# The softmax weights' row sums: adding the constant and scaling on ScalarE instead of VectorE

## The chip, the cores and the metric

The kernel runs on one core of a Trainium2 chip. The metric is the device time of one execution in microseconds; the time before is the median of three runs. One execution was also taken by the hardware profiler; its trace is what the line numbers and durations below are from.

The engines are called TensorE (PE; its weight loads are PEld), VectorE (DVE), ScalarE (ACT), GpSimd (POOL) and SyncE (SP). Each runs its own queue of instructions in order and waits for the others by semaphores.

## The reference

Causal attention with a cumulative bias, followed by a feed-forward network. Batch 8, 8 heads, 576 positions, head dimension 64; the network goes from 512 to 2048 and back, over all 4608 tokens.

```
scores = scale * q @ k.T + min(-(cum[i] - cum[j]), 0)     # causal; cum = cumsum(max(s, 0))
scores = scores - max(scores)
attn   = exp(scores)
attn   = attn / (sum(attn) + 1e-09)
x      = attn @ v                                          # heads side by side: 4608 x 512
h      = x @ w_in
g      = h if h >= 1, 0 if h <= -1, else (h + 1)**2 / 4
out    = g @ w_out
```

## The kernel before

Precision first, since it explains most of the instructions: each operand of a large product is split into a high and a low half-precision part, and three products (high-high, low-high, high-low) are added up in PSUM. The splits are the work of VectorE, ScalarE and GpSimd.

**Attention** goes by pairs of heads: 8 batches with 4 pairs each. Each pair has two jobs, one for the first 320 rows (three row tiles of 64, 128 and 128 rows) and one for the last 256 (two row tiles of 128). For each batch there come four jobs of the first kind and then four of the second. A job is cut into eight slots (`att_slot`): preparation of q and k, the score units, the loading of the next job, and, one job later, the product with v (`att_out`).

A score unit (`scores`) makes one row tile of one head: the matmuls (lines 408, or 411 and 412 from the thirteenth job on), a VectorE pass that adds the mask and finds the row's minimum (line 417), and a ScalarE exponential that also accumulates the row sum into one column of the tile `sm` (line 428). The profile shows the exponential as two instructions: the activation, and the read of the accumulator. When both heads of a row tile are there, `weights_t` turns the exponentials into weights:

- line 444, VectorE: `rs = (sums + EPS) * 2^-12` on a tile of two columns, one per head;
- line 445, VectorE: the reciprocal of `rs`;
- line 449, GpSimd: the first head's weights, times `rs`, to half precision;
- line 450, ScalarE: the second head's exponentials times `rs`, in place;
- lines 451 and 452, GpSimd: high and low part of the second head;
- line 455, VectorE: low part of the first head, and behind it SP's DMA that transposes the tile into `pt`. This last step is put off (`late`) until behind the next score minimum.

There are 32 pairs with 5 row tiles, so 160 calls of `weights_t`.

**The feed-forward network** goes over steps of one batch half and one of 16 blocks of 128 hidden columns. `ffn_h` makes 12 matmuls into PSUM (line 528), a ScalarE ReLU (line 540), two VectorE passes (543, 544), a ScalarE copy to half precision (554) and a GpSimd subtraction (555); `ffn_y` makes 12 matmuls into four accumulating banks (line 567).

**The weights** come as pairs of 32-bit words. `Weights.decode` and `Weights.split` rebuild and split them on ScalarE, VectorE and GpSimd (lines 200 to 237) while the first attention jobs and the first FFN steps run; line 207 is a ScalarE identity activation with a bias tile. The second weights' loads (`wor`) reuse buffers that the decoding frees.

**The order on each engine** isn't the program's. The kernel is built with a planner (`schedule_with_timeline_sim=True`) that simulates the engines and picks, among the instructions that are ready in its simulation, by program order and by the priorities that the kernel gives (`tc.high_priority` for lines 417, 485, 486, 540 to 555 and 581, and for the second weights' decoding). The result is a fixed queue for each engine.

Of the kernel before, what the change touches and what calls it, by code (L numbers as in the profile page):

```python
# [9 lines left out]
F32 = mybir.dt.float32  # L10
# [4 lines left out]
AF = mybir.ActivationFunctionType  # L15
ALU = mybir.AluOpType
# [6 lines left out]
P = 128  # L23
# [9 lines left out]
EPS = 1e-9  # L33
# [40 lines left out]
def attention_ffn(ctx: ExitStack, tc: tile.TileContext, qT, kT, vT, s, w_in, w_out, yT):  # L74
    nc = tc.nc
    LOADQ, CUMQ, FIRSTQ = nc.sync, nc.scalar, nc.sync
    V, A, G, T = nc.vector, nc.scalar, nc.gpsimd, nc.tensor

    cp = ctx.enter_context(tc.tile_pool(name="cp", bufs=1))
# [7 lines left out]

    floor_bias = cp.tile([P, 1], F32, name="floor_bias")
    V.memset(floor_bias, -31.0 / 64.0)

    def pow2floor(out, in_, least):
        V.tensor_scalar(out, in_, least, None, ALU.max)
        V.tensor_scalar(out.bitcast(I32), out.bitcast(I32), 0x7F800000, None, ALU.bitwise_and)
# [218 lines left out]
    raws, pts_, vts, pbs, sums = {}, {}, {}, {}, {}  # L312
# [80 lines left out]
    def scores(n, i, hd, c0, c1):  # L393
# [37 lines left out]
        if hd:  # L431
            weights_t(n, i)

    def weights_t(n, i):

        off, R, W = QT[i]
        hf = 0 if i < 3 else 1
        h_off, N, tiles = HALF[hf]
        if i == tiles[0]:
            pts_[n, hf] = ap.tile([P, 4 * (tiles[-1] + 1), N], F16, tag="pt", bufs=2, name=f"pt{n}_{hf}")  # L440
        PT = pts_[n, hf]
        PB = ap.tile([P, i + 1, 4, P], F16, tag=f"pb{hf}", name=f"pb{n}_{i}")
        rs = ap.tile([P, 2], F32, tag="rs", bufs=4, name=f"rs{n}_{i}")
        V.tensor_scalar(rs[:R], sums.pop((n, i))[:R], EPS, 2.0 ** -12, ALU.add, ALU.mult)
        V.reciprocal(rs[:R], rs[:R])  # L445
        tiles2 = pbs.pop((n, i))
        pv, pw = (Pt[:R, :W + D].rearrange("p (j c) -> p j c", c=P) for Pt in tiles2)
        his, los = ([PB[:R, :, 2 * hd + l, :] for hd in range(2)] for l in range(2))
        G.tensor_scalar(his[0], pv, rs[:R, :1], 1.0, ALU.mult, ALU.mult)  # L449
        A.activation(tiles2[1][:R, :W], tiles2[1][:R, :W], AF.Copy, scale=rs[:R, 1:])  # L450
        G.tensor_scalar(his[1], pw, 1.0, 1.0, ALU.mult, ALU.mult)  # L451
        G.tensor_tensor(los[1], pw, his[1], ALU.subtract)  # L452

        def rest():
            V.scalar_tensor_tensor(los[0], pv, rs[:R, :1], his[0], ALU.mult, ALU.subtract)  # L455
            nc.sync.dma_start_transpose(
                out=PT[:, :4 * (i + 1), off - h_off:off - h_off + R],
                in_=PB[:R].rearrange("p j g c -> p (j g c)"),
            )

        late.append(rest)
# [226 lines left out]
```

## Time and profile before

| | before |
|---|---|
| median of three runs | 1112.76 us (1111.5 to 1112.82) |
| the profiled execution: time | 1112.3 us |
| the profiled execution: span of the trace | 1110.2 us |
| mean granted TensorE clock | 0.982 |
| softmax row tiles (calls of `weights_t`) | 160 |

The span goes from the first to the last instruction; the 2.1 us between span and time lie around it. A row of a group reads: line, engine, operation, written tile <- read tiles, shapes, count | busy us, mean ns of one | idle time of the engine just before them, and what ended it. A row of a stretch gives, for each engine, the busy time in that stretch and the number of instructions. "The chain" is the work that ended last, followed back from the last instruction: at each step to what released it, or to the instruction before it on its engine; "issue" in it is time in which the engine waited for nothing that the profile shows.

### The profile page before, as it was taken

To read this page: it belongs to the slowest core of one execution; us is meant where nothing else is said; L and a number is where in the kernel's file an instruction comes from. 1 tells how busy PE (TensorE), PEld (TensorE's weight loads), DVE (VectorE), ACT (ScalarE), POOL (GpSimd) and SP (SyncE) were. 2 spreads that over 40 slices of the span, in tenths; PEclk is the share of its full clock that TensorE was granted. 3 is DMA by queue.
4 is the path that set the end of the run, shared out by engine and by line. 5 is a ranking of instruction groups with operands and counts; after the bars stand their busy time and mean duration, and the time that the engine had idled before them with its cause. 6 is when DMAs were issued, how large, how long until landed. Compare 5 with 4: busy or idle time off the path is not lost.

```text
span 1110.2 us, 25043 instructions
## 1 busy us (share of the span) xinstructions
PE 999.0 (90%) x8470; PEld 771.2 (69%) x8470; DVE 855.0 (77%) x2392; ACT 715.9 (64%) x1683; POOL 657.2 (59%) x1161
## 2 busy tenths in 40 slices
PE   0454799899999999999999999999999999899998
PEld 0132466588767877777777877787777877787787
DVE  7979987578868877878787877787777886887533
ACT  3647766467557775777567775877576755777432
POOL 3666275676647664766566755766476665765522
PEclk9997899699999999999999999999999999999999
DMA  8984536767638763987558763977387874666300
GB/s 257 241 174 129 186 78 126 140 120 152 127 84 187 165 151 72 181 164 158 106 119 186 156 149 74 193 155 167 68 178 155 170 129 80 152 156 138 68 24 20
DMA packets 339623, 153.70 MB, mean 138 GB/s; under 512 B 290728, under 2 KB 321320, under 8 KB 339496
## 3 DMA queue, kind: packets, MB, share of 16 engines
q1 hardware_dynamic: 329792, 142.17, 60.2%
q10 hardware_dynamic: 9704, 9.93, 2.9%
q8 instruction: 67, 1.10, 0.4%
q14 instruction: 60, 0.49, 0.1%
HBM read 71.00 MB, written 9.73 MB: 73 GB/s over the span
## 4 chain that ended last, share of the span: by engine, by line
PE 61%; DVE 15%; DMA 7%; POOL 7%; issue 6%; ACT 4%; ACTq 0%; DVEq 0%; SPq 0%; POOLq 0%
PE h L528 25%; PE y L567 24%; PE px L474 4%; DMA pt<-pb 4%; PE s L411 3%; DVE pb L455 3%; PE s L412 3%; DVE p L417 2%; POOL pb L449 2%; DVE Q1s L362 1%; ACT u L540 1%; PE s L408 1%; DMA wor<-in_moe_w_out_dram 1%; POOL pb L452 1%; DVE h L543 1%
## 5 line engine op out<-in xcount | busy, mean ns | idle before, releaser
L528 PE MATMUL h<-x,WI 128*128 128x256 f16 (+1 forms) x3072 | 463.5, 290 | 22.2 <-DVE u L544 19.6
L567 PE MATMUL y<-g,WO 128*128 128x256 f16 (+1 forms) x3072 | 453.0, 287 | 8.4 <-POOL g L555 6.5
L528 PEld LDWEIGHTS <-WI 128*128 128x128 f16 x3072 | 291.2, 99 | 116.3 <-issue 27.9
L567 PEld LDWEIGHTS <-WO 128*128 128x128 f16 x3072 | 288.1, 98 | 93.4 <-issue 13.8
L555 POOL TENSOR_TENSOR g<-u,g 128x320 f16<-128x320 f32 (+1 forms) x256 | 204.5, 799 | 161.2 <-ACT g L554 156.1
L428 ACT ACTIVATE p<-p,mn 64x64 f32<-64x64 f32 (+4 forms) x320 | 179.5, 561 | 140.2 <-DVE mn L417 123.0
L540 ACT ACTIVATE u<-h,ub,us 128x320 f32<-128x320 f32 (+1 forms) x256 | 149.3, 583 | 121.6 <-PE h L528 119.7
L543 DVE SCALAR_TENSOR_TENSOR h<-h,ws,u 128x320 f32<-128x320 f32 (+1 forms) x256 | 132.4, 517 | 96.9 <-ACT u L540 94.4
L449 POOL TENSOR_SCALAR pb<-p,rs 64x128 f16<-64x128 f32 (+4 forms) x160 | 95.3, 595 | 173.3 <-DVE rs L445 108.0
L452 POOL TENSOR_TENSOR pb<-p,pb 64x128 f16<-64x128 f32 (+4 forms) x160 | 169.1, 1057 | 9.3
L455 DVE SCALAR_TENSOR_TENSOR pb<-p,rs,pb 64x128 f16<-64x128 f32 (+4 forms) x160 | 132.3, 827 | 44.9 <-POOL pb L449 44.7
L417 DVE CUSTOM_DVE_ANT_0 p<-s,mask 64x64 f32<-64x64 f32 (+4 forms) x320 | 134.6, 421 | 33.5 <-PE s L412 17.4
L544 DVE SCALAR_TENSOR_TENSOR u<-u,r,h 128x320 f32<-128x320 f32 (+1 forms) x256 | 130.2, 509 | 6.2
L411 PE MATMUL s<-K1s,Q1s 128*128 128x288 f32 (+4 forms) x312 | 117.5, 378 | 11.4 <-DVE Q1s L362 7.1
L450 ACT ACTIVATE p<-p,rs 64x64 f32<-64x64 f32 (+4 forms) x160 | 89.5, 559 | 58.9 <-DVE rs L445 57.7
L554 ACT CAST g<-u 128x320 f16<-128x320 f32 (+1 forms) x256 | 108.1, 422 | 9.8 <-DVE u L544 9.1
L451 POOL TENSOR_SCALAR pb<-p 64x128 f16<-64x128 f32 (+4 forms) x160 | 93.9, 587 | 11.8 <-ACT p L450 10.0
L412 PE MATMUL s<-K2s,Q2s 68*128 68x288 f32 (+4 forms) x312 | 95.9, 307 | 1.1 <-DMA K2s<-cumd 0.7
L474 PEld LDWEIGHTS <-vt 128*64 128x64 f16 x1536 | 74.0, 115 | 32.9 <-issue 17.9
L474 PE MATMUL px<-pt,vt 128*64 128x256 f16 (+3 forms) x1536 | 84.1, 262 | 10.8 <-DMA pt<-pb 6.8
L411 PEld LDWEIGHTS s<-K1s,Q1s 128*128 128x128 f32 (+1 forms) x312 | 56.6, 181 | 21.2 <-issue 6.7
L363 DVE TENSOR_TENSOR K2s<-rk,K1s 64x1152 fp32r<-64x1152 f32 (+1 forms) x52 | 59.1, 1136 | 2.2 <-ACT K1s L360 0.9
(123 smaller groups left out, 963.3 us busy)
## 6 DMA issues: line engine op xcount, KB each, us to landing
rk<-in_k_dram SPq DMA_DIRECT2D x56, 288.0 KB
v<-in_v_dram SPq DMA_DIRECT2D x32, 288.0 KB
wir<-in_moe_w_in_dram SPq DMA_DIRECT2D x16, 512.0 KB
wor<-in_moe_w_out_dram SPq DMA_DIRECT2D x16, 512.0 KB
rk<-in_k_dram SPq DMA_DIRECT2D x48, 160.0 KB
rq<-in_q_dram SPq DMA_DIRECT2D x48, 160.0 KB
rq<-in_q_dram SPq DMA_DIRECT2D x56, 128.0 KB
out_dram<-o ACTq DMA_DIRECT2D x32, 160.0 KB
```

What stands on the lines that cost most here:

```text
L411: T.matmul(sc[:R, :c1 - c0], Q1[:, hd, qo:qo + R], K1[:, hd, c0:c1], start=True, stop=False)
L417: ttr[0] = V.tensor_tensor_reduce(out=Pt[:R, c0:c1], in0=sc[:R, :c1 - c0], in1=mask[:R, mo:mo + c1 - c0], scale=-0.125, scalar=3.0e38 if m ...
L428: A.activation(Pt[:R, :W], Pt[:R, :W], AF.Exp, bias=m2[:R], scale=-1.0, accum_out=sums[n, i][:R, hd:hd + 1])
L452: G.tensor_tensor(los[1], pw, his[1], ALU.subtract)
L455: V.scalar_tensor_tensor(los[0], pv, rs[:R, :1], his[0], ALU.mult, ALU.subtract)
L474: T.matmul(px[hd * D:(hd + 1) * D, lo:N], VT[:, vl * NB + j, hd * D:(hd + 1) * D], PT[:, 4 * j + 2 * hd + pl, lo:], start=(m == 0), stop=( ...
L528: T.matmul(h[:, :N], WI[4 * kt + ft // 4][:, wl, ft % 4 * P:(ft % 4 + 1) * P], x[:, kt, xl], start=(n == 0), stop=(n == 3 * NKT - 1),)
L540: first = A.activation(u, h[:, :N], AF.Relu, bias=ubi[b], scale=usc[b]).ins
L543: V.scalar_tensor_tensor(h[:, :N], h[:, :N], wsc[b], u, ALU.mult, ALU.max)
L544: V.scalar_tensor_tensor(u, u, r, h[:, :N], ALU.min, ALU.mult)
L555: G.tensor_tensor(g[:, 1], u, g[:, 0], ALU.subtract)
L567: T.matmul(ys[b, hf, m][:, :N], WO[8 * (m // 2) + ft // 2][:, wl, c0:c0 + P], g[:, gl], start=(ft == 0 and n == 0), stop=(ft == NFT - 1 an ...
```

## The change

Line 444 moves from VectorE to ScalarE. The activation computes `identity(scale * in + bias)`, so the constant is scaled beforehand and kept in a tile of one column, which a VectorE memset fills at the start of the kernel. The reciprocal and everything behind it stay where they are. With three lines added, the lines behind it move down by three in the kernel after.

```
     floor_bias = cp.tile([P, 1], F32, name="floor_bias")
     V.memset(floor_bias, -31.0 / 64.0)
+
+    eps_bias = cp.tile([P, 1], F32, name="eps_bias")
+    V.memset(eps_bias, EPS * 2.0 ** -12)
...
         rs = ap.tile([P, 2], F32, tag="rs", bufs=4, name=f"rs{n}_{i}")
-        V.tensor_scalar(rs[:R], sums.pop((n, i))[:R], EPS, 2.0 ** -12, ALU.add, ALU.mult)
+        A.activation(rs[:R], sums.pop((n, i))[:R], AF.Identity, bias=eps_bias[:R], scale=2.0 ** -12)
         V.reciprocal(rs[:R], rs[:R])
```

## The prediction

> **What bounds the kernel now.** I read the page first (busy shares, the chain that ended last), then the busy time by stretches, the groups of instructions, the chain in two stretches and the order of time around single instructions.
>
> ```profile
> span 1110.2 us, 25043 instructions
> PE 999.0 (90%) x8470; PEld 771.2 (69%) x8470; DVE 855.0 (77%) x2392; ACT 715.9 (64%) x1683; POOL 657.2 (59%) x1161
> PE 61%; DVE 15%; DMA 7%; POOL 7%; issue 6%; ACT 4%; ACTq 0%; DVEq 0%; SPq 0%; POOLq 0%
> ...
> 0.00:240.00 240.00, 154.30 (x972) 101.75 (x973) 193.38 (x556) 144.96 (x308) 137.26 (x233) 0.91 0.67 161
> 240.00:1040.00 800.00, 778.43 (x6921) 614.34 (x6919) 637.45 (x1789) 547.78 (x1324) 501.48 (x905) 1.00 0.67 142
> ```
>
> In the stretches the columns after the length are PE, PEld, DVE, ACT, POOL, then the granted clock. The kernel has two lives. In the first 240 us PE is idle for 86 us: weights are decoded, and VectorE is busy for 193 of 240 us. From 240 to 1040 us PE is idle for only 22 of 800 us, so nothing done to another engine can win more than 22 us there. Behind 1040 us no softmax is left for the change to touch. In the middle the 22 us are not spread evenly:
>
> ```profile
> 437.00:480.00 43.00, 38.47 (x371) 31.21 (x366) 32.31 (x98) 31.23 (x85) 27.67 (x60) 1.00 0.81 157
> 480.00:560.00 80.00, 80.00 (x686) 62.37 (x685) 65.23 (x179) 52.50 (x119) 47.98 (x80) 1.00 0.63 135
> ```
>
> The attention of one batch starts near 437 us, that of the next near 560. In the first 43 us, where the attention tiles are small and many, PE loses 4.5 us; in the 80 us behind it PE loses nothing. So the change can act in two places: the first 240 us, and the start of each of the seven later batches.
>
> **The change part by part.** It takes 160 VectorE passes (line 444) away, puts 160 ScalarE activations in their place, and adds one memset.
>
> ```profile
> L444 DVE TENSOR_SCALAR rs<-sm x160: 150/169/1111, 30.1 to 1037.4; 128x2 f32<-128x2 f32 x128, 64x2 f32<-64x2 f32 x32
> L444 DVE TENSOR_SCALAR rs<-sm 128x2 f32<-128x2 f32 (+1 forms) x160 | 37.1, 232 | 29.6 <-ACT p L428 29.4
> 0.00:240.00 240.00, 10.87 (x30) 0.91 0.67 161
> L445 DVE RECIPROCAL rs<-rs x160: 143/162/167, 31.7 to 1037.6; 128x2 f32<-128x2 f32 x128, 64x2 f32<-64x2 f32 x32
> L89 DVE MEMSET floor_bias<- 128x1 f32 x1 | 0.1, 59 | 0.8 <-PEq L676 0.8
> ```
>
> The memset costs about 59 ns as line 89 does, ahead of VectorE's wait for its first load: nothing on the path. VectorE gives back 160 x 0.232 = 37 us, 10.9 of them in the first 240 us (the stretch's row, of line 444 alone). Of that, (0.232 - 0.160) x 160 = 11.5 us is no work: the pass over two columns takes 150 to 1111 ns, the reciprocal on the same tile never more than 167. What stretches it is seen here:
>
> ```profile
> 54.26 0.98 POOL L452 TENSOR_TENSOR pb<-p,pb 128x256 f16<-128x256 f32 x1
> 54.64 0.63 DVE L444 TENSOR_SCALAR rs<-sm 128x2 f32<-128x2 f32 x1
> 98.95 1.11 DVE L444 TENSOR_SCALAR rs<-sm 128x2 f32<-128x2 f32 x1
> ```
>
> The pass starts at 54.64 inside a GpSimd instruction and ends at 55.27, 0.03 us after that one does. It is held by GpSimd. The Trainium skill (SBUF — State Buffer, Who interferes with whom) says the same: tensor_scalar on VectorE can use the port pair that it shares with GpSimd, and whoever comes second is blocked for the whole instruction; the trace agrees with 0.63 us here. By that page GpSimd would also be held by up to 150 ns for each pass, an estimate of at most 24 us over its 657 us and, at its 7% of the chain, some 1.7 us more of gain; the sum below leaves this out.
>
> How much of the 37 us is on the path? In the chain, for 30 to 100 us and for 140 to 240 us:
>
> ```profile
> by line: DMA pt<-pb 18.6%; issue 13.5%; ACT WI L229 8.0%; DVE WO L208 7.6%; POOL WO L232 6.9%; DVE pb L455 6.4%; DVE WO L201 4.5%; DVE p L417 4.4%; DVE rs L444 3.8%; POOL pb L449 3.7%; POOL WI L235 3.3%; DVE WO L211 3.3%; DVE WO L202 3.2%;
> by line: PE y L567 27.3%; PE h L528 17.7%; PE s L408 12.5%; PE px L474 7.6%; DMA pt<-pb 5.2%; issue 4.7%; DVE pb L455 3.4%; DVE c L262 2.7%; DVE p L417 2.5%; ACT p L428 2.2%; DVE rs L444 1.8%; POOL pb L449 1.5%; DVE WO L201 1.2%; DVE WO L23
> 208.20 0.45 ACT p L428 x2
> 208.67 0.68 DVE rs L444
> ```
>
> 3.8% of 70 us is 2.7 us and 1.8% of 100 us is 1.8 us: together 4.5 us of line 444 in the chain before 240 us. In most of these places VectorE's queue itself is the limit, so the time goes with the pass. In a few, as at 208 us, the pass follows the exponential directly, and there the new activation stands in its place.
>
> What does the activation cost? No ScalarE instruction over two columns is in the trace. From below, reading out the exponential's sum, one column, takes 189 ns; from above, the exponential over 64 columns takes 349.
>
> ```profile
> L428 ACT ACTIVATE p<-p,mn 128x576 f32<-128x576 f32 x64 | 49.5, 774 | 39.0 <-DVE mn L417 35.0 <-DVE r L287 3.8 <-issue 0.2
> L428 ACT ACTIVATE p<-p,mn 64x64 f32<-64x64 f32 x64 | 22.4, 349 | 32.8 <-DVE mn L417 28.9 <-POOL p L403 2.3 <-DVE rs L445 0.6
> L428 ACT ACTIVATION_READ_ACCUMULATOR p<-p,mn 128x1 f32 x256 | 48.4, 189 | 0.0
> 455.68 0.19 ACT L428 ACTIVATION_READ_ACCUMULATOR p<-p,mn 64x1 f32 x1
> 455.83 0.56 ACT L540 ACTIVATE u<-h,ub,us 128x256 f32<-128x256 f32 x1
> ```
>
> (774 - 349) / 512 is 0.83 ns per column, so two columns come to 349 - 62 x 0.83 = 298 ns. I take 0.30. ScalarE instructions overlap (the one at 455.83 starts 0.04 us before the read of the sum ends; elsewhere it is 0.09), but the new one reads that sum and so must start behind it. It pushes ScalarE's next instruction back by about 0.33 us: 160 x 0.33 = 53 us, ScalarE at 64% going to some 69%. The bounds are 0.19 x 160 = 30 us and 0.35 x 160 = 56 us of ScalarE time. A gain from the activation itself is excluded, as nothing is removed from ScalarE.
>
> From the end of the exponential to the factor `rs`, where VectorE stood idle, the way was pass + reciprocal = 0.17 + 0.16 and becomes 0.30 + 0.16: 0.13 us longer; where VectorE was busy or held, it is as long or shorter. The wait moves: line 444 waited 29.4 us for the exponential, 56 times. Now the reciprocal waits there, for the activation, and VectorE's queue (the next minimum of line 417, the FFN passes 543 and 544) stands behind it by the same 0.13 us. GpSimd's line 449 and ScalarE's line 450 wait for `rs`, and no DMA is issued or moved by the change; the transposes issued behind line 455 by SP's queue come earlier or later with `rs`.
>
> No table load is added: lines 207 (identity) and 428 (exponential) both run now, and the trace has one load only.
>
> ```profile
> L207 ACT ACTIVATE wor<-wor,floor_bias 128x512 uint16<-128x512 uint8 x8 | 11.2, 1436 | 0.1
> L200 ACT ACT_TABLE_LOAD x1 | 1.3, 1283 | 0.7 <-PEq L676 0.7
> ```
>
> At the batch starts the two sides meet. In the chain from 437 to 480 us (nine softmax groups):
>
> ```profile
> by line: issue 22.5%; DVE Q1s L362 6.6%; DVE pb L455 6.3%; POOL pb L452 6.2%; POOL pb L449 5.2%; ACT u L540 5.2%; DVE vb L382 5.1%; POOL vb L372 5.1%; ACT p L428 4.8%; DVE p L417 4.6%; POOL g L555 4.1%; DVE h L543 3.6%; DVE K2s L363 3.5%; P
> ...
> 443.86 0.19 ACT p L428
> 444.05 0.52 ACT u L540
> 447.21 0.55 ACT p L428 x2
> 447.76 0.51 ACT u L540
> 455.44 0.43 ACT p L428 x2
> 456.29 0.45 ACT g L554
> 457.54 0.53 ACT p L428 x2
> 458.07 0.25 ACT p L450
> ```
>
> By shares: VectorE's named lines hold 30% and gain 9 x 0.232 = 2.1 us, so 0.6 us; ScalarE's hold 10% and lose 9 x 0.33 = 3.0 us, so 0.3 us: a gain of 0.3 us a batch, 2 us in seven. By places: four times here the chain goes from the exponential straight on to other work of ScalarE, and an activation put between them costs 4 x 0.33 = 1.3 us a batch, 9 us in seven. I take zero between -2 and +9, nearer to the shares, since only part of the chain is lost PE time (4.5 of 43 us). Where the chain is PE, from 480 to 560 us, both effects are covered by PE's backlog.
>
> The sum: -4.5 us in the first 240 us, +0.3 us for three or so places where the activation replaces the pass on the path (0.13 us longer with reciprocal, as above), 0 at the batch starts: -4.2 us. The profiled execution took 1112.3 us (span 1110.2 and 2.1 around it), 0.5 us under the median of the runs shown; from the median, 1112.8 - 4.2 = 1108.6 us.
>
> **The rivals.** First, nothing is seen (within 0.2%, 2.2 us, about what a measurement of this kernel can tell from no change). From 109 to 135 us the chain runs through four loads of the second weights of about 4 us each:
>
> ```profile
> 109.50 4.03 DMA wor<-in_moe_w_out_dram
> 130.88 3.75 DMA wor<-in_moe_w_out_dram
> ```
>
> If these loads, rather than VectorE, set when PE gets going, what is gained before them is spent waiting. For it: 15 us of them in the chain. Against it: a load starts when VectorE has freed its buffer, so it moves forward with VectorE. Time: 1112.8, at most 2 us away.
>
> Second, slower: ScalarE becomes the limit at the batch starts. The mechanism is the one counted by places, 0.33 us each in front of line 540 (the ReLU that frees the FFN's PSUM) or 554. For it: ScalarE is busy 31 of 43 us there and would be at 34, above VectorE's 30. Against it: ScalarE is 4% of the whole chain, VectorE 15%. It decides once it costs over 0.9 us a batch (4.2 + 2.2 us over seven). With all 9 us the time is 1108.6 + 9 = 1117.6. The Trainium skill (ScalarE: Activation LUTs, Rules for kernel authors) advises adding and multiplying on VectorE rather than ScalarE; by that rule this rival is the case, and the trace agrees as far as 0.30 against 0.16 us goes.
>
> Third, a different order. The queues' order comes from a planner that simulates the engines, and 160 moved instructions shift its choices: a ScalarE instruction that is ready when the sum is not yet read (the decoding of line 207 takes 1.4 us) can be put in front of the activation, and `rs` and the transposes behind it come late. One late transpose costs PE what this one does, and PE restarts at half clock:
>
> ```profile
> 198.23 5.23 DMA pt<-pb
> 200.00:205.00 5.00, 2.54 (x16) 1.37 (x17) 2.62 (x10) 2.29 (x8) 3.60 (x11) 0.50 0.90 170
> 205.00:210.00 5.00, 4.70 (x32) 3.40 (x28) 2.67 (x10) 2.18 (x8) 2.43 (x7) 0.50 1.09 150
> ```
>
> Two such gaps more, 5 us each, and no gain: 1112.8 + 10 = 1123; with the clock on its side, one gap less gives 1104. Nothing in the trace says which way the order falls.
>
> **How the numbers follow.** The forecast 0.44, no change 0.24, ScalarE as the limit 0.20, a worse order 0.12: faster 0.44, same 0.24, slower 0.32. The likeliest case alone runs from 1102 (all 10.9 us of line 444 before 240 us on the path) to 1110.5. The range must take in the second rival and part of the third: 1102 to 1120, with 0.08 above for the third rival's worst and 0.07 below.
>
> **What would show it.** Right: line 444 is a ScalarE group x160 near 300 ns, VectorE's busy time falls by 35 to 37 us and ScalarE's rises by 45 to 55; PE's idle time before 240 us is 82 instead of 86 us; the start of each batch is as long as before. Wrong: waits of line 445 for the activation well above 29 us, line 540 waiting behind line 444 while its matmul is done, PE losing over 5.4 us in the first 43 us of a batch, or a new wait for the transposes. VectorE alone giving back 37 us proves nothing, because most of it lies beside PE.

## The result and the profile after

The kernel after takes 1143.76 us (1142.03 to 1146.43) where the kernel before took 1112.13 us on the same chip: ratio 1.0286, interval 1.0259 to 1.0312. It is 31.6 us slower. The forecast was 1108.6 us, and the range ended at 1120.

From the page of the kernel after: span, busy times and the chain that ended last by engine; under them the busy time in three stretches (PE, PEld, DVE, ACT, POOL, granted clock, DMA share, GB/s).

```profile
span 1144.6 us, 24879 instructions
PE 1012.2 (88%) x8470; PEld 777.2 (68%) x8470; DVE 838.2 (73%) x2233; ACT 758.1 (66%) x1843; POOL 658.3 (58%) x1161
PE 59%; DMA 11%; DVE 10%; POOL 7%; ACT 6%; issue 5%; ACTq 1%; SPq 0%; DVEq 0%; POOLq 0%
...
0.00:240.00 240.00, 152.73 (x937) 99.55 (x938) 184.73 (x515) 149.25 (x328) 136.56 (x224) 0.90 0.67 160
240.00:1040.00 800.00, 758.88 (x6653) 597.06 (x6653) 604.03 (x1612) 560.41 (x1408) 483.25 (x886) 0.99 0.66 137
```

The loss isn't at the start, where the gain was expected: PE is idle for 87 us of the first 240, as before. It is in the middle: from 240 to 1040 us PE is idle for 41 us where it was 22, and gets through 6653 matmuls where it was 6921. And the same 8470 matmuls keep PE busy for 13 us longer, at a mean granted clock of 0.972 instead of 0.982. DMA's share of the chain goes from 7 to 11%, VectorE's from 15 to 10%.

The rows of the activation, of the reciprocal behind it, and of who waits for them (engine, tile and line that wait <- those waited for: us in all, times, longest us):

```profile
L447 ACT ACTIVATE rs<-sm,eps_bias x160: 251/294/311, 28.9 to 1072.1; 128x2 f32<-128x2 f32 x128, 64x2 f32<-64x2 f32 x32
L448 DVE RECIPROCAL rs<-rs x160: 142/156/167, 30.3 to 1072.4; 128x2 f32<-128x2 f32 x128, 64x2 f32<-64x2 f32 x32
DVE rs L448 <- ACT rs L447: 16.6, 22, 3.4
POOL pb L452 <- DVE rs L448: 144.2, 107, 4.1
POOL pb L452 <- DMA pt<-pb: 27.0, 16, 3.5
```

GpSimd's same two waits in the kernel before:

```profile
POOL pb L449 <- DVE rs L445: 108.0, 67, 3.7
POOL pb L449 <- DMA pt<-pb: 12.6, 12, 2.6
```

The activation costs what was estimated (0.294 us), and VectorE waits less for it (16.6 us) than it waited for the exponential before (29.4 us). But GpSimd waits 144 us for the factor, where it was 108, and 27 us for transposes to free its buffers, where it was 12.6. (GpSimd is no less busy for being rid of the pass: 658 us, 657 before, and 658.5 with the pass left out in the order of before. The prediction had set aside up to 24 us here.) TensorE's waits of over 0.5 us in one batch, 20 to 40 us behind that batch's start at 697 us (in brackets: the idle time and what ended it):

```profile
721.79 0.21 PE L415 MATMUL s<-K2s,Q2s 68*64 68x64 f32 x1 [1.02 <-ACT x L488]
...
724.51 0.97 PE L570 MATMUL y<-g,WO 128*128 128x320 f16 x6 [0.61 <-ACT g L557]
...
730.85 0.94 PE L477 MATMUL px<-pt,vt 128*64 128x320 f16 x18 [1.55 <-DMA pt<-pb]
735.76 0.49 PE L570 MATMUL y<-g,WO 128*128 128x256 f16 x3 [1.38 <-POOL g L558]
```

No single wait stands out: each of the chains that feed TensorE is a little late. That looks like a different order of the work rather than one dear instruction. And the order did change: against the kernel before, 1655 of TensorE's 8398 matmuls, 570 of VectorE's instructions and 304 of GpSimd's stand elsewhere in their queue (those outside the longest sequence that both queues share). Only 61 of the 160 activations stand directly behind their exponential.

### The profile page after: what moved, and what is told of

It is laid out like the page before. It is cut to its first block, busy times and chain, and to the rows that moved or that the text cites. A ratio compares the mean times of both kernels' runs of the same rounds, so it can differ in the third digit from the quotient of the medians.

```text
span 1144.6 us, 24879 instructions
## 1 busy us (share of the span) xinstructions
PE 1012.2 (88%) x8470; PEld 777.2 (68%) x8470; DVE 838.2 (73%) x2233; ACT 758.1 (66%) x1843; POOL 658.3 (58%) x1161
## 4 chain that ended last, share of the span: by engine, by line
PE 59%; DMA 11%; DVE 10%; POOL 7%; ACT 6%; issue 5%; ACTq 1%; SPq 0%; DVEq 0%; POOLq 0%
PE y L570 25%; PE h L531 24%; DMA pt<-pb 4%; PE px L477 3%; PE s L414 3%; DMA vt<-vb 3%; PE s L415 3%; DVE pb L458 2%; DMA wor<-in_moe_w_out_dram 2%; ACT p L431 2%; DVE p L420 2%; POOL pb L452 1%; PE s L411 1%; POOL pb L455 1%; POOL g L558 1%
## 5 line engine op out<-in xcount | busy, mean ns | idle before, releaser
L531 PEld LDWEIGHTS <-WI 128*128 128x128 f16 x3072 | 292.1, 100 | 118.9 <-issue 29.4
L452 POOL TENSOR_SCALAR pb<-p,rs 64x128 f16<-64x128 f32 (+4 forms) x160 | 98.7, 617 | 174.5 <-DVE rs L448 144.2
L458 DVE SCALAR_TENSOR_TENSOR pb<-p,rs,pb 64x128 f16<-64x128 f32 (+4 forms) x160 | 136.1, 850 | 59.2 <-POOL pb L452 58.9
L454 POOL TENSOR_SCALAR pb<-p 64x128 f16<-64x128 f32 (+4 forms) x160 | 89.2, 557 | 4.3 <-ACT p L453 3.5
L366 DVE TENSOR_TENSOR K2s<-rk,K1s 64x1152 fp32r<-64x1152 f32 (+1 forms) x52 | 64.2, 1234 | 5.2 <-ACT K1s L363 4.1
```

The lines of the kernel that those rows point to most:

```text
L531: T.matmul(h[:, :N], WI[4 * kt + ft // 4][:, wl, ft % 4 * P:(ft % 4 + 1) * P], x[:, kt, xl], start=(n == 0), stop=(n == 3 * NKT - 1),)
```

## The experiments

Two theories: (A) the activation's time on ScalarE costs, in any order (the prediction's second rival); (B) the planner's new order costs, whatever runs in it (the third rival). To part them, a kernel's queues are *held*: after the program is traced, edges without a semaphore chain each engine's instructions in a listed order, so that the planner has no choice left (`queue_as` in the edits; its last argument says whether the program has the new memset). No run holds the kernel before with nothing else changed; the nearest, with one VectorE pass more, took 1.0004 of its time, so holding as such costs nothing that shows. In the held kernels and others made from the kernel before, lines keep the numbers of before unless said otherwise (leaving line 444 out moves what follows it up by one). Ratios are to the kernel before on the same chip.

**The change in the order of before.** Each activation is put directly behind its exponential; `eps_bias` is filled as in the change, here and in all runs with the activation.

```
-        V.tensor_scalar(rs[:R], sums.pop((n, i))[:R], EPS, 2.0 ** -12, ALU.add, ALU.mult)
+        A.activation(rs[:R], sums.pop((n, i))[:R], AF.Identity, bias=eps_bias[:R], scale=2.0 ** -12)
...
+        queue_as(tc, QUEUES, True)      # each queue in the order of before
```

> The change, with every engine's queue held in the order that the kernel before had; the activation stands directly behind its exponential. Theory O (the planner's new order costs the 31.6 us): 1106 to 1118 us, since 160 x 0.33 us more ScalarE work lies beside PE and 160 x 0.23 us less VectorE work is left. Theory A (the activation itself, its 53 us of ScalarE and its longer way to rs, costs it whatever the order): 1135 to 1145 us. Half each: near 1128.

1124.8 us, ratio 1.0097 (1.0063 to 1.0131): between the two bands.

**The computation of before in the order of after.** The VectorE pass stands in front of its reciprocal.

```
+        queue_as(tc, QUEUES, False)      # each queue in the order of after
```

> The kernel before (pass on VectorE, directly in front of its reciprocal), with every queue held in the order that the kernel after has. Theory O: 1138 to 1150 us, as slow as the change with no activation at all. Theory A: 1108 to 1118 us, as the activation is gone.

1149.12 us, ratio 1.0310 (1.0282 to 1.0338). So the new order is bad even with nothing moved to ScalarE. But the first run says that the activation isn't free in the good order either.

**Line 444 left out, order of before and free.** The reciprocal reads the sums themselves; constant and factor are missing.

```
-        V.tensor_scalar(rs[:R], sums.pop((n, i))[:R], EPS, 2.0 ** -12, ALU.add, ALU.mult)
-        V.reciprocal(rs[:R], rs[:R])
+        V.reciprocal(rs[:R], sums.pop((n, i))[:R])
...
+        queue_as(tc, QUEUES, False)      # in the first of the two runs only
```

> The kernel before in its own order, with line 444 left out: the reciprocal reads the sums, so the constant and the factor 4096 are missing from the weights. It measures what the pass itself is worth with the order held. By my prediction's sum at least 4.2 us and by all of line 444 before 240 us 10.9: 1101 to 1108 us. If the pass lies beside other work: 1110 to 1114 us.

Held: 1110.17 us, ratio 0.9966 (0.9948 to 0.9983).

> Line 444 left out (the constant and the factor 4096 are missing from the weights) and the planner free. In its queues the attention stands 0.1 to 0.3 FFN steps earlier than in the kernel before, where in the changed kernel it stands 0.6 to 0.9 later. If the planner's order costs by where it puts the attention: 1103 to 1113 us. If any order other than the one before is bad: 1125 to 1150 us.

Free: 1106.56 us, ratio 0.9926 (0.9905 to 0.9948). The pass on VectorE is worth 0.34% in the held order, about 4 us (2 to 6 by the interval): the size of the gain that was forecast. On this run's chip the kernel before took 1113.37 us, so 1110.17 is 3.2 us less, short of the 4.2 that the expectation's first band starts from. The profiled executions of the two don't show it (spans of 1110.2 and 1110.4 us); it rests on the medians. Free, the planner turns less work into a slightly better order.

**Line 444 left out, order of after.** The same edit, the queues as in the kernel after.

> Line 444 is left out (constant and factor with it), all queues held in the order of the kernel after. Theory that the order itself costs, whatever runs in it: 1130 (1144 less the 14 us that leaving the activation out brought in the held old order) to 1147 (1149 less the 2 us of the VectorE pass). Rival, that the order costs only because the extra operation stands in it: 1108 to 1116.

1140.86 us, ratio 1.0251 (1.0231 to 1.0272). This settles theory B: with one and the same set of instructions, the order alone makes 0.9966 into 1.0251, some 30 us (27.8 between the two profiled spans). For line 444 left out in the order of before, and then of after: the span, the stretch from 240 to 1040 us, and the transposes on TensorE (`row_m`) with which two batches following each other start.

```profile
span 1110.4 us, 24739 instructions
240.00:1040.00 800.00, 779.76 (x6895) 615.05 (x6893) 613.99 (x1653) 549.29 (x1318) 501.19 (x900) 0.99 0.68 141
L107 PE MATMUL row_m<-ident,mt x2: 272/272/273, 673.1 to 794.1; 128*1 128x128 f32 x2
```

```profile
span 1138.2 us, 24771 instructions
240.00:1040.00 800.00, 764.68 (x6703) 601.75 (x6701) 601.50 (x1617) 540.36 (x1290) 482.28 (x886) 0.99 0.66 138
L107 PE MATMUL row_m<-ident,mt x2: 273/273/273, 692.6 to 818.2; 128*1 128x128 f32 x2
```

That batch takes 121.0 us in the one order and 125.6 in the other. Where in the batch, the same pair cut at 20, 40, 60 and 70 us behind its start:

```profile
673.10:693.10 20.00, 20.00 (x170) 14.93 (x168) 14.07 (x52) 11.02 (x28) 10.08 (x16) 1.00 0.30 69
693.10:713.10 20.00, 17.95 (x179) 14.83 (x178) 15.71 (x47) 16.60 (x47) 13.15 (x32) 1.00 0.90 191
713.10:733.10 20.00, 19.77 (x199) 17.04 (x197) 16.30 (x48) 14.68 (x41) 14.08 (x34) 1.00 0.85 179
733.10:743.10 10.00, 10.00 (x95) 8.59 (x90) 8.78 (x21) 7.33 (x18) 9.57 (x15) 1.00 0.65 149
```

```profile
692.60:712.60 20.00, 20.00 (x172) 15.09 (x170) 14.41 (x50) 10.11 (x25) 8.61 (x13) 1.00 0.33 63
712.60:732.60 20.00, 16.02 (x149) 12.76 (x147) 15.67 (x43) 16.16 (x45) 15.05 (x34) 0.91 0.83 187
732.60:752.60 20.00, 20.00 (x194) 17.68 (x193) 15.30 (x49) 15.06 (x43) 13.89 (x32) 1.00 0.83 183
752.60:762.60 10.00, 9.04 (x88) 7.32 (x86) 8.55 (x17) 6.61 (x16) 6.48 (x14) 1.00 0.63 148
```

Idle time of PE goes from 2.3 to 4.9 us (stretch less busy time, over the four rows), and in the second row the clock falls to 0.91, by estimate another (1 - 0.91) x 20 = 1.8 us. Together 2.7 + 1.8 = 4.5 of the 4.6 us. So the order costs in two places of this batch: while the first attention jobs run, and once more 60 to 70 us behind the start. From the third batch on, all six show both: from 20 to 40 us PE is idle for 2.6 to 5.0 us at a clock of 0.83 to 0.91 (in the order of before for 1.1 to 3.4 us, at 1.00 in four of the six), and from 60 to 70 us for 0.7 to 1.9 us (in the order of before for none). The six batches that have a next one to measure to, the second to the seventh, are each 3.2 to 4.6 us longer, 23.3 us together; 4.0 us are lost before the second batch starts. What ends the idle times of over 0.5 us in the order of after:

```profile
716.91 0.22 PE L412 MATMUL s<-K2s,Q2s 68*64 68x64 f32 x1 [1.02 <-ACT x L484]
...
719.69 1.76 PE L566 MATMUL y<-g,WO 128*128 128x320 f16 x6 [0.67 <-ACT g L553]
...
730.67 0.49 PE L566 MATMUL y<-g,WO 128*128 128x256 f16 x3 [1.43 <-POOL g L554]
755.67 0.44 PE L411 MATMUL s<-K1s,Q1s 128*128 128x448 f32 x1 [0.96 <-DVE Q1s L362]
```

These are nearly the waits of the kernel after, without its activation.

**Does the activation itself do it, or the longer way to the factor?** The pass stays and the activation is done besides, into a tile that nothing reads; once held, once free.

```
+        spare = ap.tile([P, 2], F32, tag="spare", bufs=4, name=f"spare{n}_{i}")
+        A.activation(spare[:R], sums[n, i][:R], AF.Identity, bias=eps_bias[:R], scale=2.0 ** -12)
         V.tensor_scalar(rs[:R], sums.pop((n, i))[:R], EPS, 2.0 ** -12, ALU.add, ALU.mult)
```

> The kernel before in its own order, pass on VectorE kept, and the activation put in as well, directly behind its exponential, writing a tile that nobody reads. It separates the two costs of the activation in the held order (1124.8 against 1110.2 us without any pass). If its ScalarE time costs it (some 0.33 us each): 1122 to 1130 us. If the longer way from the exponential to rs costs it: 1111 to 1116 us, as rs comes as before.

Held: 1129.28 us, ratio 1.0137 (1.0094 to 1.0179). The factor's way is as short as before, and yet the cost is there: the activation standing in ScalarE's queue costs, not the longer way to the factor.

> The VectorE pass stays and the activation is done besides, into a tile that nothing reads; the planner orders freely. In its queues attention stands some 0.3 to 0.5 FFN steps later than in the kernel before (0.6 to 0.9 in the kernel after). Theory that the planner's answer to 160 more ScalarE instructions is what costs, whether the factor waits for them or not: 1129 (the same work in the held order) plus about half of 19, 1135 to 1148. Rival, that the bad order comes only from the longer way to the factor (exponential, activation, reciprocal): the held order's time, 1124 to 1131.

Free: 1144.59 us, ratio 1.0276 (1.0254 to 1.0298), 15 us over the held order.

**Does only work on ScalarE upset the planner?** The pass on VectorE is done twice, the first time into an unread tile.

```
+        V.tensor_scalar(spare[:R], sums[n, i][:R], EPS, 2.0 ** -12, ALU.add, ALU.mult)
         V.tensor_scalar(rs[:R], sums.pop((n, i))[:R], EPS, 2.0 ** -12, ALU.add, ALU.mult)
```

> The same work as in the run beside it, with all queues held in the order of the kernel before and the added pass directly in front of line 444. Both theories: one pass is worth 2 us in this order (1112.1 against 1110.2 with it left out), so a second gives 1112 to 1118. The rival, that a second pass costs as much as the activation did in this order: 1121 to 1127.

Held: 1114.58 us, ratio 1.0004 (0.9989 to 1.0019).

> The kernel before, with the pass of line 444 done twice on VectorE (the first into a tile that nothing reads), ScalarE untouched, planner free. In its queues attention stands some 0.35 to 0.45 FFN steps later than in the kernel before, as with the extra activation. Theory 1, that the planner answers any added work in the attention chain with an order that costs: 1130 to 1145. Theory 2, that only work added to ScalarE does this: 1112 to 1120.

Free: 1129.17 us, ratio 1.0135 (1.0118 to 1.0152), a little under that theory's band. The added work is free, the planner's answer to it costs 15 us. It isn't ScalarE alone that upsets the plan. All four wholly free plans with the activation or an added pass came out worse than before (1.0286, 1.0276, 1.0135 and, below, 1.0265); the one plan with the pass taken away came out better (0.9926, and once more below).

**The planner's answer: can a priority or a part of the order mend it?** Four tries. First, the activation gets the priority that the FFN's steps have.

```
+        with tc.high_priority(offset=FFN_LEAD):
+            A.activation(rs[:R], sums.pop((n, i))[:R], AF.Identity, bias=eps_bias[:R], scale=2.0 ** -12)
```

> The change with the planner free, but with the priority of the FFN's lines given to the activation, so that other ScalarE work goes in front of it less often. If the loss comes from the activation being queued late behind the exponential: 1112 to 1125 us. If it comes from the order of the other instructions, another draw of the order: anywhere from 1110 to 1150 us.

1143.58 us, ratio 1.0265 (1.0234 to 1.0295): no. Second, the planner's queues, compared as lists, showed that in the kernel after the attention's instructions stand behind 0.6 to 0.9 FFN steps more than before, on TensorE, GpSimd and VectorE alike. Holding ScalarE's queue alone in the order of before brings that back to within 0.1 step:

```
+        queue_as(tc, QUEUES, True)      # ScalarE's queue only, order of before
```

> The change, with only ScalarE's queue held in the old order (activation directly behind its exponential), all other queues as the planner then chooses; the attention stands where it stood before, within 0.1 FFN step, though some 1000 matmuls and 250 VectorE instructions are in other places than in the kernel before. If the position of the attention is what costs: 1120 to 1128 us, as with all queues held. If the exact old order is needed: 1135 to 1150 us.

1155.26 us, ratio 1.0377 (1.0333 to 1.0420). The theory that this lag is the cost falls. Third, the kernel after, activation and all, in its own order but for SP's queue (loads and transposes), which is held as before:

```
+        queue_as(tc, QUEUES, True)      # the order of after, SP's queue in the order of before
```

> The changed kernel with all queues as they are, but SP's (the loads and the transposes) in the old order. If the order of the transposes costs the time: 1125 to 1135 us. If it is the order of the engines' own work: 1140 to 1148 us.

1165.0 us, ratio 1.0461 (1.0421 to 1.0501), above both bands, and worse than either order whole (1.0097 and 1.0286 with the activation). In both tries a queue of the old order did worse beside queues that weren't planned with it. Fourth, the change in the old order up to about 240 us, free behind:

```
+        queue_as(tc, QUEUES, True)      # the first 12 to 24% of each queue, order of before
```

> The change, with each queue held in the order of the kernel before up to about 240 us (12% of TensorE's queue, 24% of VectorE's, 19% of ScalarE's, 20% of GpSimd's and SP's) and free behind. Theory 1, that each batch's own order costs (3 to 8 us at each of the seven): the start gains some 5 us against the kernel after, the batches stay, 1136 to 1143. Theory 2, that the start sets an offset which all batches carry: the old order goes on, 1121 to 1129.

1140.32 us, ratio 1.0230 (1.0209 to 1.0252). The loss isn't carried over from the start; the planner makes it again in the batches.

**Where the activation costs in the good order.** In the held order of before, without line 444 and with the activation, TensorE's idle time differs above all 90 to 100 us behind a batch's start (none without, 6.6 us over four batches with it), where ScalarE copies four output tiles `o` out of PSUM and its queue issues their DMAs. ScalarE and its sequencer (ACTq) without line 444, then with the activation:

```profile
760.13 0.83 ACT L580 ACTIVATE o<-y,ys 128x256 f32<-128x256 f32 x2
760.63 0.37 ACTq L581 DMA_DIRECT2D out_dram<-o  x1
760.85 0.47 ACT L580 ACTIVATE o<-y,ys 128x256 f32<-128x256 f32 x1
...
761.21 0.78 ACT L428 ACTIVATE p<-p,mn 128x576 f32<-128x576 f32 x1
761.88 0.20 ACT L428 ACTIVATION_READ_ACCUMULATOR p<-p,mn 128x1 f32 x1
...
762.84 0.47 ACT L580 ACTIVATE o<-y,ys 128x256 f32<-128x256 f32 x1
```

```profile
768.81 1.20 ACT L581 ACTIVATE o<-y,ys 128x256 f32<-128x256 f32 x3
769.89 0.78 ACT L428 ACTIVATE p<-p,mn 128x576 f32<-128x576 f32 x1
770.55 0.20 ACT L428 ACTIVATION_READ_ACCUMULATOR p<-p,mn 128x1 f32 x1
770.79 0.30 ACT L444 ACTIVATE rs<-sm,eps_bias 128x2 f32<-128x2 f32 x1
770.80 0.37 ACTq L582 DMA_DIRECT2D out_dram<-o  x1
...
774.73 0.47 ACT L581 ACTIVATE o<-y,ys 128x256 f32<-128x256 f32 x1 [2.35 <-DMA out_dram<-o]
...
775.26 0.57 PE L567 MATMUL y<-g,WO 128*128 128x320 f16 x3 [1.00 <-ACT o L581]
```

In both queues the first three copies stand in front of the exponential, and their DMA issues behind it and behind the cast that follows it (line 361). Without the activation the first one goes out at 760.63, 0.58 us before that exponential starts: the sequencer runs ahead of the engine. With the activation between them it goes out at 770.80, when the sum has been read and the activation starts, 0.91 us behind the exponential's start; the same happens in the batches around it. There are three buffers for `o`, so the fourth copy waits for the first DMA, 2.35 us, and TensorE for that copy, 1.00 us. So a fourth buffer should take this away:

```
-O_BUFS = 3
+O_BUFS = 4
```

> The change in the held order of before, with four buffers for the output tiles instead of three. Theory that the activation costs partly because it holds back the output DMAs' issue and so the buffers: TensorE's 4.3 us of waits for line 581 and what restarts behind them go, some 6 us (TensorE's idle time 90 to 100 us behind a batch's start, four places of 1.6 us), 1117 to 1121 where it was 1124.8. Rival, that these waits only move to the next place: 1123 to 1127.

1116.48 us, ratio 1.0020 (1.0006 to 1.0033), where it was 1.0097: 8.6 us less, a little more than the 6 expected. What ScalarE waited for ahead of line 581, and who waited for it, with three buffers and then with four:

```profile
  DMA out_dram<-o: 10.2, 6
  PE y L567: 2.6, 3
who waited for it (us, times):
  PE y L567: 4.3, 4
```

```profile
  PE y L567: 2.6, 3
  issue: 0.2, 1
who waited for it (us, times):
```

> Line 444 left out (constant and factor with it), the held order of before, four buffers for the output tiles instead of three. Both theories: the buffers are no limit here (0.6 us of waits), 1108 to 1112 as with three. If the fourth buffer were a gain by itself: under 1107.

Without line 444 the fourth buffer brings nothing: 1112.06 us, ratio 0.9984 (0.9969 to 0.9999), against 0.9966 with three. So of the activation's cost in this order (1.0097 - 0.9966 = 1.3%, 15 us) most was one kind of wait, behind late DMA issues; 1.0020 - 0.9984 = 0.36%, 4 us, are left. By the intervals the first difference is uncertain by some 4 us and the second by 2. The run with pass and activation both has the same waits (9.5 us, 6 times), so the same cause is likely there.

**A version that beats both.** Neither engine needs to do line 444: the factor goes into the scale that the attention's output gets anyway, and the constant 1e-9 is less than half the last digit of a sum of at least 1 in 32 bits.

```
-        V.tensor_scalar(e, csc[b], r, 2.0 ** -12, ALU.mult, ALU.mult)
+        V.tensor_scalar(e, csc[b], r, 1.0, ALU.mult, ALU.mult)
...
-        V.tensor_scalar(rs[:R], sums.pop((n, i))[:R], EPS, 2.0 ** -12, ALU.add, ALU.mult)
-        V.reciprocal(rs[:R], rs[:R])
+        V.reciprocal(rs[:R], sums.pop((n, i))[:R])
```

> Line 444 is left out, and its factor 2^-12 is taken into the output's scale (line 275: 1.0 instead of 2^-12); the constant 1e-9 is dropped, which a sum of at least 1 swallows in 32 bits anyway. The planner orders freely. Theory (the operation's time plus the order that the planner makes of it): this is the kernel with line 444 left out, 1106.6 before; expected 1104 to 1110, ratio 0.993 to 0.997. Rival (that run's gain came from other numbers in the tiles or by chance): 1112 or more.

1104.11 us, ratio 0.9917 (0.9901 to 0.9932), a little better than expected. It runs the same instructions in the same order as the free run with line 444 left out (0.9926), so the two are one plan, timed twice. From 240 to 1040 us PE is busy for 787.1 us, idle for 13 where it was 22.

## Why the prediction was wrong

The account, by ratios: leaving the pass out takes 0.34% off (1 to 0.9966), the planner's new order adds 2.85% (0.9966 to 1.0251), the activation in that order adds 0.35% (1.0251 to 1.0286). In microseconds of 1112: -4, +32, +4. The last term isn't clear of noise, as the two intervals overlap.

- **The first 240 us, -4.5 us.** The mechanism is right, and shown in the held order: the start of the second batch (`row_m`) moves from 190.0 us to 187.3 with the activation, a gain of 2.7 us, and to 187.1 with line 444 left out. In the kernel after it is at 192.6: the new order takes the gain back. Even in the held order the lead didn't last in the trace without line 444: 3.3 us at the third batch's start, 1.1 at the fourth's, none at the fifth's (552.0 against 551.9). From 20 to 40 us behind the third start TensorE's clock is 0.83 there, and 1.00 in the kernel before. The rows of before, of the change in the order of before (with its first stretch, in which PE is idle for 82.7 us; the mark was 82), and of after:

```profile
L107 PE MATMUL row_m<-ident,mt x1: 270/270/270, 190.0 to 190.0; 128*1 128x128 f32 x1
```

```profile
L107 PE MATMUL row_m<-ident,mt x1: 270/270/270, 187.3 to 187.3; 128*1 128x128 f32 x1
0.00:240.00 240.00, 157.34 (x993) 104.25 (x994) 187.97 (x532) 155.85 (x344) 139.37 (x236) 0.93 0.69 163
```

```profile
L110 PE MATMUL row_m<-ident,mt x1: 270/270/270, 192.6 to 192.6; 128*1 128x128 f32 x1
```

- **The activation's price, 0.30 us, and the places where it replaces the pass, +0.3.** Right in size: 0.294 us, and ScalarE's busy time rose by 42 us, just under the 45 to 55 given. VectorE's fell by only 17 of the 35 to 37 us forecast. Part of the difference is that other passes grew in the new order: line 363 (366 after) from 59.1 to 64.2 us, line 455 (458 after) from 132.3 to 136.1. With line 444 left out in the held order it fell by 28: busy time counts only once what two instructions overlap, and the group's 37 us overlap their neighbours (added up one by one, VectorE's instructions fell by 39 us there).
- **The batch starts, zero between -2 and +9.** The step that chose "nearer to the shares" failed: in the held order the activation cost 1.3%, 15 us, more than the upper end. The sentence behind it that was wrong is "no DMA is issued or moved by the change". The activation does move the outputs' DMAs, by holding back what stands behind it in ScalarE's queue; this place lies 90 us behind a batch's start, where the prediction had said that PE's backlog covers everything. Without it 4 us remain, inside the bounds given. The Trainium skill (ScalarE: Activation LUTs, Rules for kernel authors) advises VectorE for additions and products; the held order agrees with it, 4 us for the pass and 15 for the activation, but the other runs don't. With a fourth output buffer the activation costs 4 us as well, and in the order of after the pass costs 7 (1.0251 to 1.0310), which is no less than the activation's 4, within the noise.
- **The third rival, a different order, 0.12 and 1123 at most.** This is the step that failed and decides. The rival was named, with its mechanism (late `rs`, late transposes, a restart at a lower clock), but left out of the sum, and its price was worked out as two more gaps of 5 us, once. The order costs again in batch after batch: 4.0 us before the second batch starts and 3.2 to 4.6 us in each of the six from the second to the seventh, 27.8 us between the spans. The prediction's own rows had the stretch in which TensorE has no backlog, and that it comes seven times. Of the mechanism, the late factor and the late transposes show as GpSimd's waits in the kernel after and the lower clock in both runs of the new order; but of TensorE's four waits shown for it only one ends with a transpose.
- **The marks.** "PE losing over 5.4 us in the first 43 us of a batch" was the mark for the slow case, and it stays silent: from 448 to 491 us of the kernel after PE is idle for 4.5 us, as before. The loss there is in the clock, 0.92 instead of 1.00, and in the 80 us behind it, where PE is idle for 3.4 us instead of none. The waits of the reciprocal for the activation, another mark, are silent too: 16.6 us, not over 29. The new wait for the transposes is the mark that spoke: 27.0 us of GpSimd's where it was 12.6, and 1.55 us of TensorE's in the batch shown.

```profile
448.00:491.00 43.00, 38.51 (x345) 30.59 (x339) 28.67 (x84) 31.02 (x89) 26.71 (x55) 0.92 0.74 150
491.00:571.00 80.00, 76.65 (x646) 59.52 (x646) 61.62 (x147) 54.79 (x130) 47.90 (x83) 0.98 0.68 139
```

What stays open: which of the moved instructions make the new order bad. The places are known (20 to 40 and 60 to 70 us behind a batch's start), but holding one queue in the old order came out worse than either order whole, so the cause couldn't be put down to one queue. And the number of plans is small: that added work came with a worse order was so four times of four here, which is no law.

## What to carry to other kernels

Where a planner fixes the queues, a moved instruction has two prices, its time and the order that comes of it, and the second can be the larger by far: hold all the queues in the old order and run the change there, and leave the instruction out in both orders, to read each by itself. An instruction put behind another on an engine's queue also stands in front of everything else that this queue issues: look for the DMAs behind it and for the buffers that they free. And before moving a small operation from one engine to another, look whether a scale elsewhere can swallow it.

## What the runs showed of the hardware

ScalarE's sequencer issued a DMA while the exponential in front of it in the queue hadn't started (0.58 us ahead in the run without line 444). With an activation in between that reads the exponential's accumulated sum it didn't: the issue came 0.91 us behind the exponential's start, within 0.01 us of that activation's. An activation over two columns with a bias tile takes 0.294 us, nearly twice the reciprocal on the same tile on VectorE (0.156 us).
